# Dummy matmuls in TensorE's idle slots of the first batch, the y ring held for them, and instruction orders searched anew, in a fused attention and MLP kernel

## Chip, cores, metric

One core of one Trainium2 chip. The metric is device time in microseconds (us) of one execution. Time before: 314.06 us, the median of 3 runs (313.15 to 314.93).

On one core, "slow" is a run over 1.5% above the fastest of the same kernel; the others are "fast". Medians below are of all runs, ratios of fast runs alone. The profile of before comes from a further run of 311.61 us, below all three. A profile's *span* is about 1.8 us shorter than the time of the same run.

## The reference

Eight batches of sliding-window attention (heads 0 to 3 plain, heads 4 to 7 dilated by 4), then an MLP with SiLU over all 4608 tokens:

```
q, k, v: (8, 8, 576, 64) f32     w_in: (512, 2048)     w_out: (2048, 512)
rel = i - j
mask_plain = (rel >= 0) & (rel < 32)                          # heads 0..3
mask_dil   = (rel >= 0) & (rel < 128) & (rel % 4 == 0)        # heads 4..7
attn = softmax(where(mask, q @ k.T / 8, -1e9));  o = attn @ v
x = o.transpose(0, 2, 1, 3).reshape(4608, 512)
h = x @ w_in;   out = (h * sigmoid(h)) @ w_out
```

## The kernel before

While it is being built, the kernel runs a small planner. Attention, first layer (L1) and second layer (L2) are generators, and `Plan` keeps a modelled clock `plan.t` and emits the next step that the model says is ready. A *ring* is its record of who uses a bank of PSUM, where matmuls write; the y ring stands for the bank of y, the output of L2. The planner makes the order of instructions; each engine then works through its list in that order, with waits on semaphores. The constants of the planner and the step orders per batch come from a search. Cuts are marked `...`.

The opening. Eight zero matmuls warm TensorE (PE) up. They read `warm`, which is not a buffer of its own: it is the raw-v buffer of batch 1, not loaded yet.

```python
warm = vraws[1].rearrange("p a h r d -> p (a h r d)")
nc.vector.memset(warm[:, :GT], 0.0)
y_warm = ps_y.tile([P, GT], F32, tag="y", name="y_warm")
for n in range(8):
    nc.tensor.matmul(y_warm, warm[:, :P], warm[:, :GT], start=True, stop=True)
```

Then **all** loads of a list are emitted, before the planning loop starts. "r1" is the load of batch 1's raw v, into the buffer behind `warm`:

```python
ORDER = "k0 r0 w0b v0 w0a w1 w2 w3 d1 p1 o0 r1 o1 o2 o3 v1".split()
for what in ORDER:
    ...
    elif kind == "r":
        issue_vraw(n)          # two DMAs into vraws[n % 2]
```

Then the planning loop. If no step is ready, the modelled clock moves on:

```python
while att or l1 or l2:
    ...
    if pick is None:
        waits += [plan.heap[0][0]] if plan.heap else []
        plan.t = max(plan.t + 0.01, min(waits))
        continue
```

The softmax here doesn't subtract the row's maximum and nothing guards it: scores larger than these inputs give would overflow.

Of the kernel before, what the change touches and what calls it, by code (L numbers as in the profile page):

```python
# [16 lines left out]
def kernel(  # L17
# [9 lines left out]
    nc = tc.nc  # L27
    B, H, S, D = q.shape
    DM, DFF = moe_w_in.shape
    P = 128  # L30
# [22 lines left out]
    XR = 3  # L53
    NA = GA * GT
    BIG = 32768.0
    ORDER = "k0 r0 w0b v0 w0a w1 w2 w3 d1 p1 o0 r1 o1 o2 o3 v1".split()
    LOAD_US = {"w": 2.57, "o": 2.57, "d": 3.2, "p": 3.0, "r": 2.3, "v": 2.57, "k0": 2.2, "r0": 1.0, "v0": 2.3, "w0a": 1.3, "w0b": 1.3}
    AT_W0 = 11.4
    BIASED = (0,)

    cpool = ctx.enter_context(tc.tile_pool(name="const", bufs=1))
# [126 lines left out]
    warm = vraws[1].rearrange("p a h r d -> p (a h r d)")  # L188
    nc.vector.memset(warm[:, :GT], 0.0)
    y_warm = ps_y.tile([P, GT], F32, tag="y", name="y_warm")  # L190
    for n in range(8):
        nc.tensor.matmul(y_warm, warm[:, :P], warm[:, :GT], start=True, stop=True)
    nc.vector.memset(warm[:, GT:], 0.0)
    nc.vector.memset(vraws[0], 0.0)
# [26 lines left out]
    for t in probs:  # L221
        c = 2 * 4 * MH
        n = PW + P - c
# [4 lines left out]
    AT, AT_WIN = {}, {}  # L228
    at = AT_W0
    for what in ORDER:  # L230
        kind, n = what[0], int(what[1])
# [126 lines left out]

    plan = Plan()
    t2 = at  # L360
    AT_DIL = {0: 6.1, 1: AT["d1"], 2: t2 + 7.0}
    AT_PLAIN = {0: 9.3, 1: AT["p1"], 2: t2 + 7.0}
    AT_VRAW = {0: 10.1, 1: AT["r1"], 2: t2 + 8.6}
    AT_VP = {0: 11.4, 1: AT["v1"], 2: t2 + 11.4}
    AT_CAST = t2 + 18.0
    AT_REST = AT["k0"]
    AT_V1 = AT["r0"]
    AT_VP1 = AT["v0"]
# [97 lines left out]
    def attention(b):  # L466
# [274 lines left out]

        if b == 0:
            order = [
                ("TA", 1, "q"), ("TA", 0, "q"), ("V", 0), ("TD", 3), ("TS", 1), ("TS", 0),
                ("TD", 0), ("TA", 0, "k"), ("TD", 2), ("TD", 1), ("TA", 1, "k"), ("S", 3),
                ("TR",), ("S", 4), ("S", 6), ("S", 0), ("S", 1), ("D", 0, 1), ("P", 1), ("S", 5),
                ("D", 0, 0), ("D", 0, 2), ("V", 1), ("P", 0), ("S", 2), ("P", 3), ("P", 2),
                ("D", 1, 1), ("P", 4), ("D", 0, 3), ("P", 5), ("XP", 0), ("XP", 1), ("D", 1, 2),
                ("XD", 0), ("D", 1, 0), ("XP", 4), ("D", 1, 3), ("XP", 5), ("XP", 2), ("XD", 1),
                ("XP", 3), ("M",), ("B",),  # L750
            ]
        elif pe_path:
            order = [
                ("N", "k"), ("TD", 3), ("TD", 0), ("TD", 2), ("V", 0), ("TD", 1), ("N", "rest"),
                ("TA", 1), ("N", "q"), ("S", 3), ("TA", 0), ("TB", 0), ("TB", 1), ("D", 0, 1),
                ("D", 0, 0), ("S", 4), ("D", 0, 2), ("S", 0), ("P", 1), ("S", 1), ("D", 0, 3),
                ("P", 2), ("P", 0), ("XP", 0), ("XP", 1), ("S", 5), ("S", 6), ("XD", 0), ("V", 1),
                ("D", 1, 3), ("XP", 2), ("S", 2), ("D", 1, 2), ("D", 1, 0), ("D", 1, 1), ("P", 3),
                ("XP", 3), ("P", 4), ("XD", 1), ("P", 5), ("XP", 4), ("XP", 5),
            ]  # L760
        else:
            order = [
                ("S", 2), ("S", 0), ("P", 1), ("S", 3), ("S", 4), ("S", 1), ("S", 5), ("P", 0),
                ("V", 0), ("P", 5), ("P", 3), ("D", 0, 3), ("V", 1), ("P", 4), ("P", 2),
                ("D", 1, 1), ("D", 1, 3), ("D", 0, 1), ("D", 0, 2), ("D", 1, 2), ("D", 1, 0),
                ("D", 0, 0),
            ]
            if pe_x:
                order.insert(order.index(("D", 0, 0)), ("XP", 0))
                order.insert(order.index(("D", 0, 0)), ("XP", 1))  # L770
                order.insert(order.index(("D", 0, 2)), ("XP", 2))
                order.insert(order.index(("D", 0, 2)), ("XP", 3))
                order.insert(order.index(("D", 1, 0)), ("XP", 4))
                order.insert(order.index(("D", 1, 0)), ("XP", 5))
                order += [("XD", 0), ("XD", 1)]
        for key in order:
            kind, a = key[0], key[1:]
            rings = ["x", "z"] + (["h", "y"] if b == 0 else ["h"] if b < 2 else [])
            x_eng = ()
            if kind == "N":  # L780
                st = Step(lambda ring, a=a: paired(*a), 0.0, (), [AT_PLAIN[b]], ("DVE",))
            elif kind == "B":
                st = Step(lambda ring: third_batch(), 0.0, (), [steps["XD", 1]], ())
            elif kind == "M":
                st = Step(lambda ring: masks_of(), 0.0, (), [steps["XD", 1]], ("DVE",))
            elif kind == "TA" and b == 0:
                st = Step(
                    lambda ring, a=a: trans_a0(ring, *a), 0.36, rings,
                    [AT_PLAIN[0]],
                )  # L790
            elif kind == "TD" and b == 0:
                st = Step(lambda ring, a=a: trans_d0(ring, *a), 0.17, rings, [AT_DIL[b]])
            elif kind == "TR":
                st = Step(lambda ring: trans_d1(ring), 0.34, rings, [AT_REST])
            elif kind == "TS":
                st = Step(lambda ring, a=a: trans_a1(ring, *a), 0.36, rings, [AT_REST])
            elif kind == "TA":
                st = Step(
                    lambda ring, a=a: trans_a(ring, *a), 0.36, rings,
                    [steps["N", "k"], steps["N", "rest"]], ("ACT",),  # L800
                )
            elif kind == "TB":
                st = Step(
                    lambda ring, a=a: trans_b(ring, *a), 0.18, rings, [steps["N", "q"]], ("ACT",)
                )
            elif kind == "TD":
                st = Step(lambda ring, a=a: trans_d(ring, *a), 0.28, rings, [AT_DIL[b]], ("DVE",))
            elif kind == "S":
                if not pe_path:
                    deps = [turned[b]]  # L810
                elif b == 0:
                    plain = [("TA", hp, nm) for hp in range(HP // 2) for nm in "kq"]
                    rest = [("TS", hp) for hp in range(HP // 2)]
                    dil = [("TD", h) for h in range(HN)]
                    keys = (plain, plain, plain + rest, dil, dil, dil + [("TR",)], dil + [("TR",)])
                    deps = [steps[key_] for key_ in keys[a[0]]]
                elif a[0] < 3:
                    deps = [steps[t, hp] for t in ("TA", "TB") for hp in range(HP // 2)]
                else:
                    deps = [steps["TD", h] for h in range(HN)]  # L820
                st = Step(
                    lambda ring, a=a: scores(ring, *a), 0.17 + 0.32 * (b in BIASED), ["s"] + (["hh"] if b < 2 else []),
                    deps + readers.get(base + a[0] - NP, []), ("ACT",) if b in BIASED else ("ACT", "DVE"),
                )
            elif kind == "V":
                st = Step(lambda ring, a=a: vd_of(*a), 0.0, (), [AT_V1 if b == 0 and a[0] else at_vraw], ())
            elif kind == "P":
                us = sorted({home["p", a[0], hp][0] for hp in range(HP // 2)})
                st = Step(
                    lambda ring, a=a: av_p(ring, *a), 0.13, rings,  # L830
                    [AT_VP1 if b == 0 and a[0] > 2 else at_vp] + [steps["S", u] for u in us],
                    ("DVE",),
                )
            elif kind == "D":
                us = sorted({home["d", a[0], a[1] // 2, h][0] for h in range(HN)})
                st = Step(
                    lambda ring, a=a: av_d(ring, *a), 0.13, rings,
                    [steps["V", a[0]]] + [steps["S", u] for u in us], ("DVE",),
                )
            elif kind == "XP":  # L840
                st = Step(lambda ring, a=a: x_p(ring, *a), 0.1, rings, [steps["P", a[0]]], x_eng)
            else:
                st = Step(
                    lambda ring, a=a: x_d(ring, *a), 0.28, rings,
                    [steps["D", a[0], r] for r in range(DIL)], x_eng,
                )
# [131 lines left out]
        l2 += [(g, st) for st in layer2(g, l1s_of[g])]  # L978

    plan.push(Step(None, 0.0), first_cast(), 0.0)  # L980
    LOOK = 8
    LIM_ATT = 1.1
    LIM_PAIR = 0.4
    LIM_L1 = 1.8
    SIDE = 0.9
    NEAR = 1.0
    SPARE = 6
    seconds = {st.mate for _, st in att if st.mate}
    side = 0.0
    while att or l1 or l2:  # L990
# [31 lines left out]
        if pick is None and g2 < SPARE and l2[0][1].rings and plan.backlog(l2[0][1].uses) <= 9.0:  # L1022
            l2[0][1].rings = ["y", "x", "z"]
            r = plan.ready(l2[0][1])
            if r is not None and r <= plan.t:
                pick = l2, l2[0]
        if pick is None:
            waits += [plan.heap[0][0]] if plan.heap else []
            plan.t = max(plan.t + 0.01, min(waits))
            continue  # L1030
# [37 lines left out]
```

## Time and profile before

| reading (view) | before |
|---|---|
| time, median | 314.06 us |
| profiled span (page) | 309.8 us |
| PE busy (page) | 299.4 us, 97% |
| first L1 matmul (timeline of PE) | 22.40 us |
| half clock in the first batch (windows) | about 9.0 to 15.8 us |
| PE's waits for xR (waits, line below) | 0.2 us |

```profile
PE h L892 <- DMA xR<-x_s: 0.2, 1, 0.2
```

The head of the page, with the granted PE clock in 40 slices of the span (9 is 90% or more):

```profile
span 309.8 us, 6177 instructions
...
PE 299.4 (97%) x2402; PEld 155.5 (50%) x2402; DVE 195.8 (63%) x498; ACT 164.7 (53%) x318; POOL 54.5 (18%) x86
...
PEclk9599999999999999999999999999999999999999
```

PE is the bound, and the second slice shows a loss of clock. The timeline of PE in that stretch (start, duration, instruction, and in brackets the idle time before it and what ended it):

```profile
1.19 3.59 PE L192 MATMUL y_warm<-vraw 128*128 128x512 f16 x8 [1.19 <-DVE vraw L189]
5.16 0.26 PE L557 MATMUL td<-ident_w,nat 96*128 96x96 f16 x1 [0.37 <-DMA nat<-in_k_dram]
6.17 0.81 PE L557 MATMUL td<-ident_w,nat 96*128 96x96 f16 x15 [0.75 <-DMA nat<-in_q_dram]
...
9.71 0.85 PE L582 MATMUL ta_q<-ident_w,nat 96*64 96x96 f16 x16 [1.97 <-DMA nat<-in_q_dram]
```

PE waits three times for k and q. The windows of the same stretch; the columns are the window, its length, busy time and count of each engine, PE's clock, DMA:

```profile
8.00:10.00 2.00, 0.29 (x8) 0.29 (x10) 0.00 (x0) 0.43 (x1) 1.55 (x4) 0.75 1.72 170
...
12.00:14.00 2.00, 2.00 (x26) 0.99 (x20) 0.67 (x3) 1.06 (x3) 1.86 (x3) 0.50 1.47 193
...
16.00:22.40 6.40, 5.50 (x105) 3.83 (x104) 5.51 (x22) 5.24 (x15) 3.65 (x6) 1.00 1.32 202
```

The clock is halved from about 9 to 15.8 us, while PE is busy. That is what the change goes after.

### The profile page before, as it was taken

How to read it: one execution, taken by the hardware profiler on the slowest of the kernel's cores; microseconds unless marked ns; L12 is line 12 of the kernel's file. 1: busy time of each engine (PE TensorE's matmuls, PEld its weight loads, DVE VectorE, ACT ScalarE, POOL GpSimd, SP SyncE). 2: the span in 40 equal slices, each digit the busy share in tenths (PEclk: the TensorE clock that was granted, in tenths of full speed). 3: DMA queues.
4: the chain of work that ended last, by engine and by line, in shares of the span. 5: the costliest groups of instructions: out<-in, count | busy, mean ns of one | idle time of the engine just before them, and what ended most of it. 6: DMA issues, size and time to landing. Idle time of an engine off the chain costs nothing.

```text
span 309.8 us, 6177 instructions
## 1 busy us (share of the span) xinstructions
PE 299.4 (97%) x2402; PEld 155.5 (50%) x2402; DVE 195.8 (63%) x498; ACT 164.7 (53%) x318; POOL 54.5 (18%) x86
## 2 busy tenths in 40 slices
PE   6789989999999999999999999999999999999995
PEld 2468855555545544554445444544454444444444
DVE  6389998699868735794589457854795355355000
ACT  7478872667573626444653456436643455355111
POOL 8855723001900005000500050000000000000000
PEclk9599999999999999999999999999999999999999
DMA  8999999998999849999999899964116500000222
GB/s 104 179 203 197 197 190 201 204 192 164 142 190 218 183 121 154 217 184 190 127 210 221 196 138 205 223 166 114 44 56 152 89 36 34 34 36 0 79 91 71
DMA packets 107382, 44.55 MB, mean 144 GB/s; under 512 B 73304, under 2 KB 102872, under 8 KB 107352
## 3 DMA queue, kind: packets, MB, share of 16 engines
q0 software_dynamic: 48528, 19.86, 52.7%
q1 hardware_dynamic: 53496, 14.91, 25.4%
q10 hardware_dynamic: 5328, 9.37, 8.7%
q8 instruction: 19, 0.31, 0.4%
q14 instruction: 11, 0.09, 0.1%
HBM read 39.81 MB, written 18.28 MB: 188 GB/s over the span
## 4 chain that ended last, share of the span: by engine, by line
PE 85%; DVE 5%; DMA 5%; ACT 3%; issue 1%; POOL 1%; ACTq 0%; DVEq 0%; POOLq 0%
PE y L925 38%; PE h L892 36%; PE s L632 3%; PE av_d L677 3%; DMA nat<-in_q_dram 2%; PE av_p L677 2%; DMA xR<-x_s 1%; DVE probs L650 1%; DMA x_s<-oD 1%; DVE gT L903 1%; PE s L620 1%; ACT probs L641 1%; ACT ob L938 1%; ACT kqD L510 1%; DVE oP L681 1%
## 5 line engine op out<-in xcount | busy, mean ns | idle before, releaser
L925 PE MATMUL y<-w_out,gT 128*128 128x512 f16 (+1 forms) x592 | 137.8, 373 | 0.0
L901 ACT ACTIVATE th<-h 128x512 f32<-128x512 f32 (+1 forms) x160 | 88.9, 557 | 78.3 <-PE h L892 69.0
L903 DVE SCALAR_TENSOR_TENSOR gT<-th,h 128x512 f16<-128x512 f32 (+1 forms) x160 | 99.2, 629 | 48.0 <-ACT th L901 47.5
L892 PEld LDWEIGHTS <-w_in 128*128 128x128 f16 x640 | 59.1, 97 | 52.5 <-issue 1.5
L925 PEld LDWEIGHTS <-gT 128*128 128x128 f16 x592 | 55.1, 98 | 57.5
L892 PE MATMUL h<-xR,w_in 128*128 128x512 f16 x320 | 77.6, 379 | 0.2 <-DMA xR<-x_s 0.2
L892 PE MATMUL h<-xA,w_in 128*128 128x512 f16 (+1 forms) x320 | 62.1, 336 | 0.0
L938 ACT ACTIVATE ob<-y 128x512 f32<-128x512 f32 (+1 forms) x36 | 21.3, 591 | 42.6 <-PE y L925 42.6
L641 ACT ACTIVATE probs<-s 128x768 f16<-128x768 f32 (+2 forms) x32 | 24.7, 772 | 12.2 <-PE s L632 10.5
L677 PEld LDWEIGHTS <-probs 128*128 128x128 f16 x448 | 22.0, 98 | 16.3 <-DVE probs L650 3.0
L681 DVE TENSOR_TENSOR oD<-av_d,rcps 72x256 f16<-72x256 f32 x64 | 26.9, 420 | 2.2
L650 DVE TENSOR_TENSOR probs<-probs,mask_p 128x768 f16<-128x768 f16 x21 | 11.5, 551 | 22.6 <-ACT probs L641 22.6
L681 DVE TENSOR_TENSOR oP<-av_p,rcps 96x256 f16<-96x256 f32 x48 | 20.2, 421 | 1.6
L427 POOL COPY fence<-kqT 128x1 f16<-128x1 f16 x10 | 2.3, 232 | 92.9 <-DMA kqT<-kq_s 92.9
L645 ACT ACTIVATE probs<-s 128x384 f16<-128x384 f32 (+2 forms) x38 | 17.2, 477 | 1.1 <-PE s L632 1.1
L677 PE MATMUL av_d<-vd,probs 128*128 128x65 f16 x256 | 15.4, 196 | 1.2 <-DVE oD L681 0.6
L945 DVE TENSOR_SCALAR ob<-y 128x128 f32<-128x128 f32 x1 | 0.3, 290 | 20.6 <-ACT ob L943 20.6
L680 DVE RECIPROCAL rcps<-av_d 72x4 f32<-72x4 f32 x64 | 11.0, 171 | 2.7 <-PE av_d L677 2.7
L677 PE MATMUL av_p<-vp,probs 128*128 128x65 f16 x192 | 12.0, 194 | 0.3
L165 POOL DMA_DIRECT2D vraw<-in_v_dram x16 | 10.8, 680 | 5.8 <-DVE gT L903 2.5
L650 DVE TENSOR_TENSOR probs<-probs,mask_d 128x576 f16<-128x576 f16 (+1 forms) x23 | 11.6, 512 | 0.1
L680 DVE RECIPROCAL rcps<-av_p 96x4 f32<-96x4 f32 x48 | 8.3, 172 | 5.3 <-PE av_p L677 5.3
(93 smaller groups left out, 155.0 us busy)
## 6 DMA issues: line engine op xcount, KB each, us to landing
out_dram<-ob ACTq DMA_DIRECT2D x35, 256.0 KB, 3.1
kq_s<-in_k_dram POOLq DMA_DIRECT2D x5, 576.0 KB, 9.0
kq_s<-in_q_dram POOLq DMA_DIRECT2D x5, 576.0 KB, 11.6
vp<-in_v_dram POOLq DMA_DIRECT2D x7, 384.0 KB, 7.5
w_out<-in_moe_w_out_dram POOLq DMA_DIRECT2D x4, 512.0 KB, 10.8
vraw<-in_v_dram POOLq DMA_DIRECT2D x8, 224.0 KB, 5.3
w_in<-in_moe_w_in_dram POOLq DMA_DIRECT2D x3, 512.0 KB, 9.8
x_s<-oP SPq DMA_DIRECT2D x10, 144.0 KB, 3.1
```

The lines of the kernel that those rows point to most:

```text
L165: nc.gpsimd.dma_start(out=vraw[p0 : p0 + m1 - m0, ab].rearrange("p h r d -> p h (r d)"), in_=src[m0:m1],)
L641: nc.scalar.activation(p2, both[:, :, :n], AF.Exp, scale=scale)
L645: nc.scalar.activation(p2[:, i], sp[i][:, :n], AF.Exp, scale=scale)
L650: nc.vector.tensor_tensor(p2, p2, mk, ALU.mult)
L677: nc.tensor.matmul(a[:, i, : D + 1], lhs(i), rhs(i), start=True, stop=True)
L680: nc.vector.reciprocal(rcp[:n], a[:n, :, D : D + 1])
L681: nc.vector.tensor_tensor(o, a[:n, :, :D], rcp[:n, :, None].broadcast_to([n, HN, D]), ALU.mult)
L892: nc.tensor.matmul(h[:, :w], w_in16[:, c, f * P : (f + 1) * P], x_g[:, c], start=(c == 0), stop=(c == HP - 1),)
L901: nc.scalar.activation(th[:, :w], h[:, :w], AF.Tanh, scale=0.5)
L903: nc.vector.scalar_tensor_tensor(gTs[g][:, f, :w], th[:, :w], 1.0, h[:, :w], ALU.add, ALU.mult)
L925: nc.tensor.matmul(y, gTs[g][:, f, tb * P : (tb + 1) * P], w_out16[:, f, c0:c1], start=(f == 0), stop=(f == NFF - 1),)
L938: nc.scalar.activation(ob, y, AF.Copy, scale=0.5)
```

## The change

Its intent: PE's idle slots in the first batch are filled with short dummy matmuls, so that the clock stays up. The dummies write into the opening's y bank, so the y ring is held until `WARM`. Landings were measured again, and the orders and planner limits searched anew for them. In the orders, `S` is a step of scores (q times k), `P` and `D` are steps of weights times v of the plain and of the dilated heads, `V` is a copy of v. The core of the diff, cut:

```diff
-    ORDER = "k0 r0 w0b v0 w0a w1 w2 w3 d1 p1 o0 r1 o1 o2 o3 v1".split()
+    ORDER = "k0 v0 r0 p1 w1 w0a w0b w2 w3 d1 r1 o1 o0 o2 o3 v1".split()
-    for n in range(8):
+    for n in range(9):
         nc.tensor.matmul(y_warm, warm[:, :P], warm[:, :GT], start=True, stop=True)
...  (landing times, with one of its own for the k transposes of batch 0; the orders of
...   batch 0 and of batches 1 and 2 replaced)
         else:                                   # batches 3 to 7 (comment added here)
             order = [
-                ("S", 2), ("S", 0), ("P", 1), ("S", 3), ("S", 4), ("S", 1), ("S", 5), ("P", 0),
-                ("V", 0), ("P", 5), ("P", 3), ("D", 0, 3), ("V", 1), ("P", 4), ("P", 2),
-                ("D", 1, 1), ("D", 1, 3), ("D", 0, 1), ("D", 0, 2), ("D", 1, 2), ("D", 1, 0),
-                ("D", 0, 0),
+                ("S", 0), ("S", 2), ("S", 3), ("P", 5), ("S", 1), ("S", 4), ("V", 0), ("D", 0, 0),
+                ("P", 2), ("S", 5), ("V", 1), ("D", 0, 3), ("D", 1, 2), ("P", 3), ("D", 1, 0),
+                ("D", 0, 1), ("P", 4), ("D", 1, 3), ("P", 0), ("D", 1, 1), ("D", 0, 2), ("P", 1),
             ]
...
-    LOOK = 8
-    LIM_ATT = 1.1
-    LIM_PAIR = 0.4
-    LIM_L1 = 1.8
-    SIDE = 0.9
-    NEAR = 1.0
+    LOOK = 14
+    LIM_ATT = 1.0
+    LIM_PAIR = 1.2
+    LIM_L1 = 1.4
+    SIDE = 0.7
+    NEAR = 0.3
+    WARM = 18.0
+    held = Step(None, 0.0)
+    held.done = WARM
+    plan.rings["y"].append(held)
...
         if pick is None:
+            if plan.t < WARM:
+                if 5.5 < plan.t:
+                    nc.tensor.matmul(
+                        y_warm[:, :P], warm[:, :P], warm[:, :P], start=True, stop=True
+                    )
+                plan.t += 0.056
+                continue
             waits += [plan.heap[0][0]] if plan.heap else []
```

## The prediction

> **What bounds the kernel now.** TensorE: the page gives it 97% of the 309.8 us span, the chain of waits 85%. What is left lies mostly in the first 22.4 us, before the first MLP matmul: PE waits 1.2 us for the first memset, 0.4 and 0.7 us for k and q of the dilated heads, then 2.0 us (until 9.71) for q of the plain heads. The windows show the granted clock at 0.5 from about 9.0 to 15.8 us: two windows of 3.41 us, the length that the Trainium skill, "TensorE: Matmul & The Clock Gate", Part 1, gives for the activity window; this trace agrees. At half clock eight score matmuls took 0.43 us in the chain, later 0.24.
>
> **What the change intends.** Dummies of 128 columns fill PE's waits so that the clock stays up. Work between 9.7 and 15.8 us is 6 us at half rate, so at most 3 us (1%) is to be had, plus perhaps 1 us from the new orders (PE waits about 1.3 us between 22 and 56 us).
>
> **What it also does.** The built order shows 75 new dummies; 13 stand straight after the nine opening matmuls, ahead of the first transposes. They read `warm`, which is the raw-v buffer of batch 1. The opening matmuls are emitted before that buffer's load; the new ones after it, since all listed loads are emitted before the planning loop. So the first dummy becomes a reader of batch 1's v: in the built program it waits for the fourth landing on a DMA semaphore, and that transfer is the first half of load "r1". PE is in order, so all real work queues behind it. The load waits only for the opening matmuls and eight ScalarE copies, so nothing deadlocks.
>
> **When r1 lands.** In the trace of before, the last p1 load landed at 32.85 us, then o0 at 35.5, r1's first half at 36.2. The new list has the same bytes ahead of r1 except o0 (2.6 us): estimate 33.6 us. PE idles from about 5 to 33.6 us; before, its transposes started at 5.2.
>
> **After it.** All data of batch 0 are there, but PE is cold. Estimate, from durations in the trace: 5.4 us at half clock (30 dummies, 16 transposes, one score step), 12.3 us at full clock up to the first MLP matmul (45 dummies, 2.5 us, and 1.0 us of batch 1's transposes among them), 1 to 2 us of waits for ScalarE and VectorE. First MLP matmul at about 53 us instead of 22.4. The rest (287 us) is PE bound and moves along, less 1.0 us already done and 1 us from better orders: +28.5 us.
>
> **Prediction:** 342 us, 80% range 337 to 347. Faster 0.02, within 2% 0.02, slower 0.96. The whole stall is on the critical path.
>
> **What would show each step.**
> - PE's longest wait: about 28 us before the dummies, released by a DMA into the raw v buffer at 33 to 35 us.
> - ScalarE and VectorE idle over the same stretch.
> - Granted clock 0.5 for 3.4 to 6.8 us after PE restarts, then 1.0.
> - First MLP matmul at 51 to 55 us; from there to the end 284 to 288 us.
> - Correct result: the dummies' bank is reset by its next user.
>
> **What would make it wrong.** If the fourth landing were an earlier load, PE would start sooner and the result would be 2 to 4 us better than before. If batch 0 goes faster with all its data present, the loss is nearer 24 us; if batch 2's loads, which wait for batch 0, come late, it is above 32.

## More of the kernel before

From batch 3 on, x goes through DRAM: outputs oP (plain heads) and oD (dilated) are stored to `x_s`, and once all four stores of a batch are in, a DMA transpose brings x back as `xR`, which L1 reads (PE's waits for xR: 0.2 us). These stores, and the transposes that bring in the k and q of a later batch (`nat<-kq_s`, `kqT<-kq_s`), are all issued by SP, in one list:

```python
def av_p(ring, j):                       # av_d likewise, for oD
    ...
    parts[j // 3] += 1
    if not pe_x and parts[j // 3] == 3:
        nc.sync.dma_start(out=rows[:, j - 2 : j + 1], in_=oP[:, j - 2 : j + 1]...)
        yield "DMA", 3.0
        stored(b)                        # the fourth one starts group_gen
def group_gen(g):
    nc.sync.dma_start_transpose(out=x_of(g)[:, :, GT - n :], in_=x_s[t0 : t0 + n])
```

SP's list around the stores of batch 5, the third batch that goes through DRAM (this is the issue of DMAs, not their transfer):

```profile
169.47 0.85 SPq L715 DMA_DIRECT2D x_s<-oD  x1
170.44 1.33 SPq L158 DMA_TRANSPOSE kqT<-kq_s  x1
171.86 0.85 SPq L715 DMA_DIRECT2D x_s<-oD  x1
172.80 1.80 SPq L158 DMA_TRANSPOSE kqT<-kq_s  x1
175.52 1.83 SPq L450 DMA_TRANSPOSE xR<-x_s  x1
```

and the chain of waits there:

```profile
171.86 3.64 DMA x_s<-oD
...
175.52 4.52 DMA xR<-x_s
...
180.08 1.89 PE h L892 x8
```

The last store is issued at 171.86 us, xR lands at 180.04, and PE runs out of other work at about 179.9: a tight chain with no slack. Even here the last store is late. VectorE's work that completes its data:

```profile
169.64 0.42 DVE L681 TENSOR_TENSOR oD<-av_d,rcps 72x256 f16<-72x256 f32 x1
```

The data are complete at 170.06 us, the store is issued 1.8 us later, after the transpose of 170.44.

## The result

The result is correct and slower: 348.24 us (median of 6 runs, 345.7 to 352.66; one of them slow) against 314.02 us of before in the same rounds. The ratio is 1.1056, 95% interval 1.098 to 1.1132. A ratio here is the mean time of one kernel's fast runs over that of the other's fast runs of the same rounds, so it is not quite the ratio of the medians. The prediction had the direction, the cause and the size of the stall, but 342 us with a range that ended at 347: it is 6 us short.

The head of the page after the change:

```profile
span 344.1 us, 6322 instructions
...
PE 305.5 (89%) x2478; PEld 161.4 (47%) x2478; DVE 195.3 (57%) x492; ACT 165.2 (48%) x323; POOL 54.5 (16%) x86
...
PEclk9999996999999999999999999999999999999999
```

PE is busy about as long as before (305.5 us, 6.1 more), in a span 34.3 us longer: the time is idle time. PE's longest waits (what waited for what: us in total, times, longest):

```profile
PE y_warm L1034 <- DMA vraw<-in_v_dram: 28.8, 1, 28.8
PE h L892 <- DMA xR<-x_s: 2.7, 2, 1.6
```

The timeline of PE at the start:

```profile
1.19 4.02 PE L192 MATMUL y_warm<-vraw 128*128 128x512 f16 x9 [1.19 <-DVE vraw L189]
34.05 1.57 PE L1034 MATMUL y_warm<-vraw 128*128 128x128 f16 x13 [28.84 <-DMA vraw<-in_v_dram]
35.42 1.49 PE L558 MATMUL td<-ident_w,nat 96*128 96x96 f16 x16
...
42.68 0.72 PE L1034 MATMUL y_warm<-vraw 128*128 128x128 f16 x10
43.23 0.49 PE L621 MATMUL s<-mask_p,ident_w 128*128 128x384 f16 x2
```

One single wait of 28.8 us in front of the first dummy, ended by a DMA into the raw-v buffer; the real work that used to start at 5.16 us now starts at 35.42. The 13 dummies start 105 ns apart ((35.42 - 34.05) / 13), about half the rate of the ten at 42.68 us, which start 55 ns apart ((43.23 - 42.68) / 10). Two more things were not predicted. The first is a second cold spell (windows; the seventh slice of PEclk above):

```profile
50.00:52.00 2.00, 0.65 (x12) 0.38 (x10) 1.93 (x7) 1.09 (x3) 2.00 (x3) 0.87 1.66 183
...
54.00:56.00 2.00, 2.00 (x19) 1.57 (x17) 1.26 (x5) 1.35 (x5) 0.00 (x0) 0.50 2.45 165
```

The second: waits for xR rose from 0.2 to 2.7 us. SP's list around the stores of batch 5:

```profile
201.06 2.33 SPq L158 DMA_TRANSPOSE kqT<-kq_s  x1
203.48 0.85 SPq L716 DMA_DIRECT2D x_s<-oD  x1
204.44 1.41 SPq L158 DMA_TRANSPOSE kqT<-kq_s  x1
205.94 0.53 SPq L697 DMA_DIRECT2D x_s<-oP  x1
208.48 2.00 SPq L451 DMA_TRANSPOSE xR<-x_s  x1
```

and VectorE's work that makes the data of that last store:

```profile
201.27 0.42 DVE L682 TENSOR_TENSOR oP<-av_p,rcps 96x256 f16<-96x256 f32 x1
```

oP is complete at 201.69 us and its store is issued at 205.94, 4.2 us later: it stands in SP's list behind the rest of a transpose, a store and another transpose. With the old order the last store was one of oD, and the plain half was stored early.

| | before | after | predicted for after |
|---|---|---|---|
| first half of r1 lands | 36.2 | 34.0 | 33.6 |
| first L1 matmul | 22.40 | 54.48 | 53 (51 to 55) |
| from there to PE's last matmul | 284.06 (to 306.46) | 286.28 (to 340.76) | 2 less than before |
| span | 309.8 | 344.1 | 338.3 (309.8 + 28.5) |

The 5.8 us between the two spans of the last row are, up to rounding, 0.4 from the landing, 1.1 from the first batch (20.5 us from the landing to the first L1 matmul, 19.4 predicted), and 4.2 from the rest, which was to gain 2.0 us and lost 2.2. From PE's last matmul to the end it is 3.4 us in both.

### The profile page after: what moved, and what is told of

It is laid out like the page before. It is cut to its first block, busy times and chain, and to the rows that moved or that the text cites. A ratio compares the mean times of both kernels' runs of the same rounds, so it can differ in the third digit from the quotient of the medians.

```text
span 344.1 us, 6322 instructions
## 1 busy us (share of the span) xinstructions
PE 305.5 (89%) x2478; PEld 161.4 (47%) x2478; DVE 195.3 (57%) x492; ACT 165.2 (48%) x323; POOL 54.5 (16%) x86
## 4 chain that ended last, share of the span: by engine, by line
PE 73%; DMA 15%; DVE 4%; ACT 3%; POOL 2%; issue 1%; ACTq 1%; SPq 0%; POOLq 0%
PE h L892 31%; PE y L925 30%; DMA xR<-x_s 4%; DMA vraw<-in_v_dram 3%; DMA x_s<-oP 3%; PE s L633 3%; DMA w_in<-in_moe_w_in_dram 2%; PE av_d L678 2%; DMA nat<-in_q_dram 2%; PE av_p L678 2%; PE y_warm L1034 2%; DMA kqT<-kq_s 1%; DVE gT L903 1%; ACT ob L938 1%; POOL nat L131 1%
## 5 line engine op out<-in xcount | busy, mean ns | idle before, releaser
L925 PEld LDWEIGHTS <-gT 128*128 128x128 f16 x592 | 55.8, 98 | 59.7
L892 PE MATMUL h<-xA,w_in 128*128 128x512 f16 (+1 forms) x320 | 64.2, 344 | 0.0
L1034 PE MATMUL y_warm<-vraw 128*128 128x128 f16 x75 | 6.8, 248 | 28.8 <-DMA vraw<-in_v_dram 28.8
L642 ACT ACTIVATE probs<-s 128x768 f16<-128x768 f32 (+2 forms) x33 | 25.7, 780 | 13.5 <-PE s L633 11.0
L678 PEld LDWEIGHTS <-probs 128*128 128x128 f16 x448 | 21.2, 97 | 14.6 <-DVE probs L651 2.6
L513 DVE COPY kqD<-td 128x576 f16<-128x576 f16 (+1 forms) x8 | 3.2, 416 | 29.7 <-PE td L558 29.7
L1034 PEld LDWEIGHTS <-vraw 128*128 128x128 f16 x75 | 5.5, 114 | 29.9 <-DMA vraw<-in_v_dram 29.7
L511 ACT COPY kqD<-td 128x384 f16<-128x384 f16 (+1 forms) x6 | 3.4, 568 | 31.0 <-PE td L558 30.5
L646 ACT ACTIVATE probs<-s 128x288 f16<-128x288 f32 (+2 forms) x36 | 16.8, 476 | 0.0
L178 POOL DMA_DIRECT2D vp<-in_v_dram x7 | 10.0, 1429 | 27.0 <-PE av_p L678 20.9
```

Source lines behind the costliest of these rows:

```text
L642: nc.scalar.activation(p2, both[:, :, :n], AF.Exp, scale=scale)
L646: nc.scalar.activation(p2[:, i], sp[i][:, :n], AF.Exp, scale=scale)
L678: nc.tensor.matmul(a[:, i, : D + 1], lhs(i), rhs(i), start=True, stop=True)
L892: nc.tensor.matmul(h[:, :w], w_in16[:, c, f * P : (f + 1) * P], x_g[:, c], start=(c == 0), stop=(c == HP - 1),)
L925: nc.tensor.matmul(y, gTs[g][:, f, tb * P : (tb + 1) * P], w_out16[:, f, c0:c1], start=(f == 0), stop=(f == NFF - 1),)
L1034: nc.tensor.matmul(y_warm[:, :P], warm[:, :P], warm[:, :P], start=True, stop=True)
```

## The experiments

Each ratio is to the kernel before, of the same rounds: e1 to e8 ran on one chip, e9 to e14 on another. Two runs of e1 and three of e2 lie above their slow line, most of them barely (320.44 us against 320.10, for instance), and are left out of their ratios, which may be a little low for that. "Same PE order" means that I compared the lists of real matmuls in the built programs and found them equal.

| run | what | median us | ratio (95% interval) |
|---|---|---|---|
| after | the change | 348.24 | 1.1056 (1.098 to 1.1132) |
| e1_own_tile | after, dummies read a tile of their own | 318.95 | 1.0145 (1.0078 to 1.0212) |
| e2_no_dummies | after, dummies planned, not emitted | 320.53 | 1.017 (1.0094 to 1.0246) |
| e3_one_read | before + one dummy | 339.03 | 1.0838 (1.0772 to 1.0905) |
| e4_old_orders | before + planner's dummies, own tile | 316.81 | 1.0103 (1.0037 to 1.0169) |
| e5_p_first | e1, P1 and P0 earlier in batches 3 to 7 | 314.47 | 1.0059 (1.0002 to 1.0115) |
| e6_old_steady | e1, old order of batches 3 to 7 | 317.04 | 1.011 (1.0044 to 1.0175) |
| e7_pinned | before, same PE order, dummies in place | 314.32 | 1.0061 (1.0 to 1.0123) |
| e8_act_store | e1, last oP store from ScalarE's queue | 313.41 | 1.0011 (0.9956 to 1.0066) |
| e9_stall_act | after, last oP store from ScalarE's queue | 342.72 | 1.0881 (1.0812 to 1.095) |
| e10_stall_fill | after, dummies in the waits at 50 us | 346.66 | 1.1019 (1.0967 to 1.1071) |
| e11_stall_both | e9 and e10 in one | 341.94 | 1.087 (1.0813 to 1.0927) |
| e12_before_act | before, last store of a batch from ScalarE's queue | 312.82 | 0.9945 (0.99 to 0.999) |
| e13_pinned_act | e7 and e12 in one | 313.29 | 0.9977 (0.993 to 1.0024) |
| e14_before_act_again | e12 again, beside e13 | 312.68 | 0.9954 (0.9904 to 1.0005) |

All gave a correct result.

### e1: a tile of their own

```diff
+    idle_w = cpool.tile([P, P], F16, name="idle_w")
+    nc.vector.memset(idle_w, 0.0)
...
-                        y_warm[:, :P], warm[:, :P], warm[:, :P], start=True, stop=True
+                        y_warm[:, :P], idle_w, idle_w, start=True, stop=True
```

> The changed kernel, but the 75 dummies read a zeroed tile of their own instead of batch 1's raw-v buffer; everything else as changed. Theory (false read of batch 1's v): the 28.8 us wait in front of the dummies is gone, first MLP matmul at 20 to 22.5 us, time 308 to 313 us, ratio to before 0.98 to 1.00, no half clock between 9 and 16 us. Rival (75 dummies on PE, the held y ring or the new orders cost the time): still over 330 us, first MLP matmul after 35 us.

Same PE order as after. The stall is gone, and the ratio falls from 1.1056 to 1.0145, which is 28.5 us of 313. So the false read is shown to be the stall. But the expected time is missed: 318.95 us, not 308 to 313. Something else in the change costs about 4.5 us. As expected, the clock is not halved between 9 and 16 us (it is from 23.0 to 26.5), but the first L1 matmul, expected at 20 to 22.5 us, starts at 24.72, later than in before (22.40). The longest of PE's waits in e1's profile:

```profile
PE h L894 <- DMA xR<-x_s: 4.2, 2, 3.4
```

The timeline of PE in e1, where the longer of the two waits ends:

```profile
184.23 3.18 PE L894 MATMUL h<-xR,w_in 128*128 128x512 f16 x8 [3.45 <-DMA xR<-x_s]
```

PE waits 3.45 us for xR, and the eight matmuls behind it take 3.18 us where the same eight take 1.89 elsewhere: the wait also costs the clock. In the middle e1 is level with before (the 321st of the 640 L1 matmuls starts at 149.4 us in both traces); by the 481st it is 6.2 us behind (232.1 against 225.9).

### e2: planned but not emitted

```diff
-                    nc.tensor.matmul(
-                        y_warm[:, :P], warm[:, :P], warm[:, :P], start=True, stop=True
-                    )
+                    pass
```

> The changed kernel without emitting the 75 dummies; the planner still counts their time and still holds the y ring, so all other instructions keep their order. Theory: no read of batch 1's v, so no stall; half clock back for about 6.8 us from 9 us on; 311 to 315 us. Rival (new orders or the held ring cost the time): over 330 us. Against e1 the difference is what the dummies are worth: expected 1 to 3 us in e1's favour.

No stall, which agrees. The time was expected at 311 to 315 us and is 320.53: the plan alone (orders, limits, held ring) carries the extra cost. Against e1 the dummies are worth about 0.8 us (1.017 against 1.0145), well within the intervals. The second spell of half clock, expected from 9 us on, is not in e2's profile: PE runs at half clock from the start, the clock's first record, at 9.69 us, grants the full clock, and up to 183.76 us it stays so. In e14's profile the clock is halved from the start to 13.65 us. So the loss that the change goes after differs from execution to execution.

### e3: one dummy in the kernel before

```diff
+    nc.tensor.matmul(y_warm[:, :P], warm[:, :P], warm[:, :P], start=True, stop=True)
     plan.push(Step(None, 0.0), first_cast(), 0.0)
```

> The kernel before, plus one single dummy matmul of 128 columns that reads the same buffer, emitted after the loads and before the planning loop. Theory: that one matmul waits for the first half of r1, which landed at 36.2 us in the kernel before; PE waits about 31 us in front of it, first MLP matmul at 51 to 54 us, time 340 to 348 us. Rival (it takes many dummies or the new orders): within 1 us of before, 314 us.

One matmul of 128 columns makes the kernel before 8.4% slower. The timeline of PE in e3:

```profile
35.80 0.29 PE L980 MATMUL y_warm<-vraw 128*128 128x128 f16 x1 [31.00 <-DMA vraw<-in_v_dram]
```

This is the cleanest form of the fault. The first L1 matmul starts at 50.15 us, 27.75 us late; from there to PE's last matmul it is 283.96 us against 284.06 of before. So "the rest moves along" holds to 0.1 us in these two profiles, as long as the orders are the old ones. (By the ratio, e3 loses 26.2 us.) Two sizes were missed by a little: I expected the start at 51 to 54 us and 340 us or more.

### e4: old orders, planner's dummies

```diff
-    for n in range(8):
+    for n in range(9):
...  (idle_w as in e1)
+    WARM = 18.0
+    held = Step(None, 0.0)
+    held.done = WARM
+    plan.rings["y"].append(held)
...
+            if plan.t < WARM:
+                if 5.5 < plan.t:
+                    nc.tensor.matmul(
+                        y_warm[:, :P], idle_w, idle_w, start=True, stop=True
+                    )
+                plan.t += 0.056
+                continue
```

> The kernel before with its old orders and landing times, plus the planner's dummies (87 of them) in a tile of their own, nine opening matmuls and the held y ring. Theory: no stall; the clock stays at 1.0 through 9 to 16 us, worth 1 to 3 us: 311 to 314 us. Against e1 the difference is what the new orders are worth: 0 to 2 us in e1's favour. Rival (dummies delay real work at full clock as much as they save): 314 us or more.

316.81 us, missed on the slow side: 1% over before with old orders and no stall. The first L1 matmul is earlier (20.47 us), but the order of real matmuls differs from that of before from 13.5 us on, and this profile too waits for xR, 2.5 us. A searched order is fitted to its planner: a disturbance in the first batch moved steps long after it. Which of its parts (the held ring, the dummies' time, the ninth matmul) did so was not tested.

### e5 and e6: which part of the order

e5 moves two steps in the new order of batches 3 to 7; e6 puts the old order of these batches back.

```diff
-                ("P", 2), ("S", 5), ("V", 1), ("D", 0, 3), ("D", 1, 2), ("P", 3), ("D", 1, 0),
-                ("D", 0, 1), ("P", 4), ("D", 1, 3), ("P", 0), ("D", 1, 1), ("D", 0, 2), ("P", 1),
+                ("P", 2), ("S", 5), ("V", 1), ("D", 0, 3), ("D", 1, 2), ("P", 3), ("P", 1),
+                ("P", 0), ("P", 4), ("D", 1, 0), ("D", 0, 1), ("D", 1, 3), ("D", 1, 1), ("D", 0, 2),
```

> e1 (dummies in a tile of their own) with one more edit: in the new order of batches 3 to 7 the last plain-head steps P1 and P0 are moved ahead of the last dilated-head steps, so that a store of oD and not one of oP is the last before the xR transpose. Theory (P1 last puts the last store of oP behind the kqT transposes in SP's in-order queue, so xR lands late): PE's waits for xR fall from 4.2 us to under 1 us, the second cold spell at 183 us goes too, time 4 to 6 us under e1: 310 to 314 us. Rival (the new planner limits make the late stretch slow, whatever the order): within 2 us of e1, 317 us or more.

> e1 with the old order of batches 3 to 7 put back whole (planner limits, first two orders and loads as changed). Theory (the new order of these batches causes the xR waits): waits for xR under 1 us, 310 to 314 us. Rival (new planner limits or held ring): within 2 us of e1, 317 us or more.

e5 gains about 2.7 us over e1 (1.0145 to 1.0059; the two intervals overlap, so this is barely resolved), under the 4 to 6 expected; its waits for xR are 2.0 us, not under 1. e6 gains 1.1 us, which the intervals do not separate from nothing; its waits for xR are still 2.7 us. So the form "the new order of batches 3 to 7 is the cause" falls: the old order under the new limits is no cure. What the profiles of e1, e4, e5 and e6 have in common is that xR comes late, not one list.

### e8: only the place of one store

```diff
-                nc.sync.dma_start(
+                late = parts[0] + parts[1] == NB
+                (nc.scalar if late else nc.sync).dma_start(
                     out=rows[:, j - 2 : j + 1],
```

> e1 with the same instruction order on PE; only the last store of oP of each of batches 3 to 7 is issued from ScalarE's DMA queue in place of SP's. Theory (SP's in-order queue holds that store back by 5 us behind the kqT transposes): the store is issued about 171 us instead of 176, xR lands at 180 to 181 us instead of 184, PE's waits for xR fall under 1.5 us, 2 to 5 us under e1. Rival (the store waits for its data, or the transpose itself is slow): waits for xR stay over 3 us and the time within 1 us of e1.

Same PE order as e1, and 1.0145 falls to 1.0011: 4.2 us. That the store stood in SP's list was the cost; whether through its late issue or through sharing SP's queue, no run tells apart. Its profile fell in a slow run, so I lean on the times: five of six runs are within 312.14 to 314.30 us. That profile doesn't show what was expected of it: the store is issued at 172.06 us, but xR's transpose only at 178.90 (178.56 in e1), and PE's waits for xR are 3.1 us, not under 1.5. How the gain came about is thus not shown here; e10 and e11 below show it better.

### e9, e10, e11: the same two terms in the changed kernel itself

e9 makes e8's edit in the changed kernel. e10 puts 30 dummies into the waits at 49.6 to 52.1 us, writing into the tile of the step that waits, so the plan stays:

```diff
...  (a helper `fill(flat, n, w)` that emits n dummies of w columns)
+            if (b, hp) == (1, 0):
+                fill(tps.rearrange("p i r m -> p (i r m)"), 20, P)
...
+            if b == 0 and j > 3:
+                fill(xp.rearrange("p h q -> p (h q)"), 5, QB)
```

> The changed kernel, stall and all, with one edit: the last store of oP of each of batches 3 to 7 is issued from ScalarE's DMA queue. Every matmul in the same order. Theory (of the excess over the predicted 342 us, the xR waits are one term): xR waits fall from 2.7 us to under 1 us, 2 to 4 us faster than the 348.2 us of the changed kernel, 344 to 346 us, ratio to before about 1.095. Rival (the xR waits belong to the variant without the stall only, the excess is elsewhere): within 1 us of 348.

> The changed kernel, stall and all, with 30 more dummies in the waits of PE from 49.6 to 52.1 us (5 + 5 in front of the last two plain-head output transposes, 20 in front of batch 1's first transposes), each writing into the tile of the step that waits. Theory (those waits, 1.7 us in all, bring the cold spell at 51.5 to 58.3 us, which costs up to 3.4 us): no cold spell between 42 and 70 us, 1.5 to 3.5 us faster than the changed kernel. Rival (VectorE and ScalarE hold that stretch, the clock is off the critical path): within 1 us of 348, as in e7.

> The changed kernel with both edits of the two runs above. Theory: the two terms add up, 341 to 344 us, near the predicted 342, ratio to before 1.085 to 1.095; the stall of 28 to 29 us stays. Rival: 346 us or more.

e9: 342.72 us, the predicted time, with the stall still there (28.0 us in its profile). The store now is issued as soon as its data are there; ScalarE's timeline in e9:

```profile
201.40 0.34 ACTq L698 DMA_DIRECT2D x_s<-oP  x1
```

Its data are complete at 201.37 us. But the edit takes one link out of SP's list, not the list itself: the last store to land is now one of oD, issued at 203.74 us behind a transpose, and xR's transpose starts at 207.53, only 0.95 us earlier than in after. From 1.1056 to 1.0881 is 5.5 us, more than the 2 to 4 expected. The profile of after showed only 2.7 us of xR waits, but it was one of its two fastest runs (345.94 us against a median of 348.24). e10 did remove the cold spell at 51.5 us, yet gains about 1.2 us (1.1019), which the intervals do not separate from nothing, and its profile waits 4.8 us for xR. e11 is 1.087, no better than e9 within the intervals: its time is as expected, but that the two terms add up is not shown.

The cleanest pair is e10 against e11: the same chip, the same rounds, all runs fast, the same PE order, and the store's queue the only difference. The medians are 346.66 and 341.94 us, 4.7 us apart, and the ranges (345.04 to 347.24, 340.67 to 342.62) do not touch. PE's waits for xR in e10, then in e11:

```profile
PE h L902 <- DMA xR<-x_s: 4.8, 3, 3.0
...
PE h L903 <- DMA xR<-x_s: 1.0, 3, 0.5
```

From the first L1 matmul to PE's last it is 288.20 us in e10 and 283.43 in e11. So of the 6 us that the prediction lacked, the late store is most (4.7 to 5.5); the cold spell is not a term of its own that these runs could resolve.

### e7, e12, e13, e14: what the idea is worth

e7 keeps the plan of before, adds the ninth opening matmul, and puts 13 + 30 dummies where PE waited:

```diff
+    def fill(flat, n):
+        for _ in range(n):
+            nc.tensor.matmul(flat.bitcast(F32)[:, :P], idle_w, idle_w, start=True, stop=True)
...
+            if h == 3:
+                fill(tps.rearrange("p n m -> p (n m)"), 13)
...
+            if (hp, nm) == (1, "q"):
+                fill(tps.rearrange("p r m -> p (r m)"), 30)
```

> The kernel before with its plan untouched (every real matmul in the same order), nine opening matmuls, and 13 + 30 dummies that read a tile of their own and write into the tile of the step that waits: 13 ahead of the first dilated transposes, 30 ahead of the q transposes of the plain heads. Theory (the gain in the clock is real but weights w1 to w3, which land at 21.6 to 26.8 us, and VectorE hold the first MLP stage back): clock 1.0 through 9 to 16 us, first MLP matmul 1.5 to 3 us earlier, whole kernel 0.5 to 2 us faster than before. Rival (dummies cost as much as they save): within 0.5 us of before or slower.

The clock stays up: the two mask matmuls of an S step (q times k) take 0.42 us at 10.48 us, where before the same two took 0.66 us at 11.13. The timeline of PE in e7:

```profile
10.48 0.42 PE L631 MATMUL s<-mask_d,ident_w 128*128 128x288 f16 x2
```

The first L1 matmul starts at 20.07 us, 2.3 us earlier, as expected. The kernel, expected to be 0.5 to 2 us faster, is not: 1.0061 (1.0 to 1.0123). e12 then takes the kernel before and moves only the store that completes a batch to ScalarE's queue:

```diff
...  (the same in av_p)
-                nc.sync.dma_start(out=rows, in_=oD[:, ab].rearrange("p r h d -> p r (h d)"))
+                late = sum(parts) == NB + 2 * DIL
+                (nc.scalar if late else nc.sync).dma_start(
+                    out=rows, in_=oD[:, ab].rearrange("p r h d -> p r (h d)")
+                )
```

> The kernel before, every matmul in the same order, with the store that completes each of batches 3 to 7 issued from ScalarE's DMA queue in place of SP's. The profile of before shows PE waiting only 0.2 us for xR, so if that run is typical: within 0.5 us of before. If the runs of before that are 2 to 3 us longer at the same clock owe it to that chain: 0.5 to 2 us faster and a narrower spread.

0.9945 (0.99 to 0.999), and all six runs lie within 311.82 to 313.21 us, where before, in the same rounds, ran from 311.39 to 317.56. It is the best version here, by about half a percent, and the verdict at 2% is "same". Last, e13 joins e7 and e12, with e12 run again beside it:

> e7 (plan of before, dummies in place) and e12 (completing store from ScalarE's queue) in one. If what the dummies gain early in e7 (first MLP matmul 2.3 us earlier) was given back in the xR chain: 1 to 2 us faster than e12, ratio to before 0.988 to 0.991. If the early gain is lost before that (weights, VectorE), or the cold spell is absent in most runs of before anyway: within 0.5 us of e12, ratio 0.993 to 0.997.

> e12 again, unchanged, on the same chip and in the same rounds as e13, because the difference looked for is under 1%. Expected ratio to before 0.990 to 0.999, as in e12, with runs within 1.5 us of each other.

e13 is 0.9977 and e14 0.9954, and e14's interval (0.9904 to 1.0005) no longer excludes 1: that e12 is faster than before is likely, not certain. The dummies add nothing that these runs resolve once the xR chain is shorter either. The profile of e13 shows where the early start goes. Its first L1 matmul is at 20.73 us, 0.8 us before e14's (21.52), and then it waits. Some of PE's waits in e13:

```profile
PE s L643 <- DMA kqT<-kq_s: 1.1, 1, 1.1
PE y L940 <- DMA w_out<-in_moe_w_out_dram: 1.1, 3, 0.4
PE h L907 <- DMA xR<-x_s: 0.9, 1, 0.9
```

PE idles 5.2 us in all after its first L1 matmul (sum of the gaps over 0.05 us), against 2.7 in e14's profile. Most of it ends on a DMA: weights, k and q, or x that do not come earlier because PE does. But e13's profile is of its slowest run (314.69 us) and e14's of one of its fastest (312.10): that these waits are typical was not shown.

## Why the prediction was right or wrong

- **The false read stalls PE: right.** "PE's longest wait: about 28 us before the dummies, released by a DMA into the raw v buffer at 33 to 35 us": 28.8 us, released at 34.0. e1 takes it away and gains 28.5 us; e3 makes it with one matmul.
- **ScalarE and VectorE idle over the same stretch: right**, 30.3 and 29.4 us before their first copies of the transposes.
- **First L1 matmul at 51 to 55 us: right**, 54.48. **From there to the end 284 to 288 us: wrong**, 289.7 (344.14 - 54.48).
- **Granted clock 0.5 for 3.4 to 6.8 us after the restart, then 1.0: half right.** Half rate until 37.83 us by the clock's first record, 3.8 us. Not then 1.0: a second spell from 51.5 to 58.3 us. Removing it (e10) changed the time by about 1.2 us, inside the intervals.
- **"The rest (287 us) is PE bound and moves along, less 1.0 already done and 1 us from better orders": wrong. This is the step that failed.** It had the sign of the new orders wrong. In the profile the rest, up to PE's last matmul, took 2.2 us more, not 2.0 less. What stood in its place: under the new orders and limits the store that completes x stands late in SP's list, 4.2 us after its data, and PE waits for xR. With that store on another queue and all else as changed (e9) the time is 342.72 us, the predicted number. That this fits so well is partly luck: even with the store moved and the cold spell filled (e11) the rest takes 283.43 us, 0.6 less than before, not 2.0 less. I took "searched anew" for "better" and costed only PE's list. The chain of before, with its slack of about zero at xR, and the changed order of SP's list in the built program were both at hand before.
- **"At most 3 us is to be had" from the clock: right as a bound, and too generous.** Filling the gaps did start the MLP 2.3 us earlier in a profile (e7), but no timed pair shows a gain. The bound took half clock to mean twice the time. The prediction's pair, 0.43 and 0.24 us for eight score matmuls, is of two different tiles; eight of the same tile (`kqD`) take 0.36 us at 11.79 and 0.24 at 18.63 in the chain, 1.5 times.
- **Correct result: right.**

What stays open: how much of e1's excess is the new limits and how much the held ring, since each edit moves the whole plan; and whether the cold spell at 51.5 us costs anything once the store is moved (e9 to e11 is 0.3 us by the ratios, within the intervals).

## What to carry to other kernels

A dummy instruction has dependencies like any other: give it operands that nothing else ever writes, or look in the built program for what its first instance waits on. Where a schedule is searched, it is fitted to every list at once, also those of the DMA queues; before trusting new orders, find the chain with the least slack (here last store, transpose back, first matmul) and see where its links now stand. Here one queue issued both slow transposes and an urgent small store, and taking the store off it gained 4.7 us in the changed kernel.

## What the Trainium skill lacked or had wrong

- "TensorE: Matmul & The Clock Gate", section "Why this matters for your kernels", advises no PE-idle gaps over about 3 us. Far less was enough here: in the changed kernel the 3.41 us up to 51.48 held gaps of 0.27, 0.28 and 0.54 us, and the clock was halved for the next 6.8; with those waits filled (e10) it was not. In e5's profile gaps of 0.92 and 0.16 us in a window (by its first clock record, 20.7 to 24.1 us) did not halve it, so 1.1 us in all went either way. (The page does report, further up and without sizes, a kernel whose frequent short idles made the clock oscillate.)
- The same page's caveats on the throttle's trace records do not say how to read the clock before its first record. In the changed kernel that record is at 37.83 us; the profile's windows from 34 to 38 us show 1.00 while dummies start 105 ns apart, half rate. The matmul times decide.
- The same page's advice to keep TensorE busy does not say that the clock can be off the critical path: e7 and e13 kept it up and gained nothing that the intervals show (1.0061 and 0.9977).
- "DMA: Bandwidth & Descriptors", section "Rules for kernel authors", says that spreading DMAs over SP, ACT and GpSimd "only saves sequencer issue time". That agrees with these runs, but it undersells it: SP's list held one store back by 4.2 us behind transposes that take 1.3 to 2.3 us each to issue, and moving it was worth 4.7 us (e10 to e11) and about 0.5% (e12, at the edge of its interval). The page gives no issue time for a DMA transpose of this size.
- No page that I read warns that a scratch operand borrowed from a later load's buffer becomes a reader of that load when it is emitted after it: 31.0 us of wait for one matmul (e3).
